# A pace and a spread: how much attention and weight work stand beside the first up projection

## The chip, the core and the metric

The kernel runs on one core of one Trainium2 chip. The metric is the device time of one execution in microseconds: the median of three runs of the kernel before is 1006.17 us (1006.15 to 1007.19). Lower is better.

## What is computed

Sliding-window attention with a linear position bias over 8 batches of 8 heads, 576 positions and head dimension 64, all float32. Its output, laid out as 4608 tokens of 512 features, is the input of a bilinear feed-forward layer.

```python
def _attn_ref(q, k, v):                      # (8, 8, 576, 64) each
    scores = scale * np.matmul(q, k.transpose(0, 1, 3, 2))
    bias = slopes[:, None, None] * (-np.abs(rel))[None, :, :]
    mask = (rel >= 0) & (rel < 128)
    scores = np.where(mask, scores + bias[None], -1e9)
    scores = scores - np.max(scores, axis=-1, keepdims=True)
    attn = np.exp(scores)
    attn = attn / (np.sum(attn, axis=-1, keepdims=True) + 1e-09)
    return np.matmul(attn, v)

def _moe_ref(x, w_a, w_b, w_out):            # (4608,512), (512,1536) twice, (1536,512)
    a = x @ w_a
    b = x @ w_b
    return a * b @ w_out
```

## The kernel before, in words

**Numbers.** TensorE multiplies float16 operands. Each float32 operand is scaled by a power of two and split into a high and a low float16 part, and a product is three matmuls (high by high, high by low, low by high). The weights arrive as 64-bit words, which the kernel first turns into float32 (`convert`, lines 126 to 136: ScalarE L130, VectorE L131 and L133, POOL L135), then squares for the norms (L141), then scales and splits (L149 and L150 for the up weights, L230 and L231 for the down weights).

**Batches.** Work is done batch by batch: the attention of a batch, four pairs of heads, then its up projection (two products per feature tile and their elementwise product), then its down projection. The attention of batch b + 1 is emitted beside the up and down projections of batch b. The attention of batch 0 runs alone at the start, beside the first steps of the weights.

**Attention as a generator.** `attention()` (line 658) goes through the pairs of batches 1 to 7. Pair i (i = 0 is the first pair of batch 1) has seven steps; after each it yields its place, i + 1/7, i + 2/7, ... i + 1. Within a pair stand: score matmuls (L374 for batch 1, L378 later) with VectorE's bias and minimum (L382) and ScalarE's exponential (L383), in four groups of 3, 2, 2 and 2 pieces; the normalization (L392, L396, ScalarE L399, VectorE L400); the DMA transpose of the probabilities on SP's queue (L405); for the pair before, the split of v (ScalarE L295, VectorE L296) and the product with v (L501), its eviction (L414) and squares (L420, L429 and POOL's addition L430); for the next pair the squares of q and k (L321), their split (L338, L339), four copies on SP's queue (L347 to L350) and the load of the pair after it (L304, L305 for batch 1; L311, L312 later). After the fourth pair of a batch its hidden state is split (L435, L436) and scaled (L515 to L522).

**Pace.** `Pace` (lines 957 to 971) runs the attention along another generator. `to(place)` steps the attention until its last yield is at or above the place; `along(main, n, place)` goes from the place where attention stands to `place` in n even parts, one at each yield of `main`:

```python
            start = max(self.at, 0)
            for k, _ in enumerate(main, 1):
                self.to(start + (place - start) * k / n)
                yield
```

**The first batch.** `first_up` (line 776) yields 48 times and once more: 12 feature tiles by two halves of the tokens by two weights, each a group of twelve matmuls (L836) into one of five PSUM banks. ScalarE copies the first product out (L783), VectorE multiplies it with the second (L785), which frees the banks; then the result is split (L829, L830, on POOL for the last six tiles). `first_down` (line 804) yields 24 times: two halves of the tokens by 12 tiles, each twelve matmuls (L812), and at the end of each half four evictions (L820, L822).

**The weights.** `up_weights` (line 165, 56 yields) and `down_weights` (line 204, 27 yields) are chained in one generator, `weights`. The first attention takes 24 of its steps. `weave` (line 949) gives a side generator `steps` steps, spread evenly over the yields a to z of the main one. The 71st step of the chain computes the scales of the down weights (L226), and each of the next twelve splits one tile of them.

**Order.** In the first batch only SP's queue keeps the order in which it is written (`manual_schedule(engines=SP)`); the other engines' instructions are put in order by the framework's scheduler, with priorities in the order of writing (a few instructions carry a higher one). From batch 1 on TensorE's order is the written one.

Of the kernel before, what the change touches and what calls it, by code (L numbers as in the profile page):

```python
# [46 lines left out]
def attention_then_bilinear_ffn(ctx: ExitStack, tc: tile.TileContext, qT, kT, vP, w_a, w_b, w_out, rel, slopes2, outT):  # L47
# [11 lines left out]
    def bank(name):  # L59

        pl = next(banks)
        return pl.tile([P, 512], F32, tag="ef" if pl is ps_ef else "ch", name=name)
# [710 lines left out]
    def new_hidden():  # L773
        return work.tile([P, 2, HT], F32, tag="rc", name="rc", bufs=3)

    def first_up(st, h):

        late = []
        hid = {}

        def keep(f, t, m, ps):
            if m == 0:
                act.copy(hid[f][:, t, :], ps[:, 0:HT])  # L783
            else:
                vec.scalar_tensor_tensor(out=hid[f][:, t, :], in0=hid[f][:, t, :], scalar=st.g, in1=ps[:, 0:HT], op0=ALU.mult, op1=ALU.mult)  # L785
                if t:
                    halve(hid.pop(f), f, h, pool if f >= NF // 2 else vec)

        for f in range(NF):
            hid[f] = new_hidden()  # L790
            for t in range(2):
                for m in range(2):
                    ps = bank("up_ps")
                    terms(ps, (f, 3 if m else 0), B12 if t else 0, True, False)
                    terms(ps, (f, 2 if m else 1), 2 if t else 1, False, True)
                    late.append((f, t, m, ps))
                    if len(late) > 2:
                        keep(*late.pop(0))
                    yield
        for x in late:  # L800
            keep(*x)
        yield

    def first_down(b, oi, h):

        started["down"] = b
        for t in range(2):
            pss = [bank("dn_ps") for _ in range(NE)]
            for f in range(NF):
                for e in range(NE):  # L810
                    for n, (wi, hi) in enumerate(((0, 0), (0, 1), (1, 0))):
                        pe.matmul(pss[e][:, 0:HT], wdn[:, f, wi, e * P:(e + 1) * P], h[:, f, t, hi, :], start=(f == 0 and n == 0), stop=(f == NF - 1 and n == 2))  # L812
                yield

            more = new_hidden()
            for e in range(NE):
                o = row() if e < 2 else more[:, e - 2, :]
                with tc.high_priority(offset=PRIO):
                    if e % 2:
                        vec.tensor_scalar(out=o, in0=pss[e][:, 0:HT], scalar1=oi, scalar2=None, op0=ALU.mult)  # L820
                    else:
                        act.activation(o, pss[e][:, 0:HT], AF.Copy, scale=oi)  # L822
                act.dma_start(outT[e * P:(e + 1) * P, b * S + t * HT:b * S + (t + 1) * HT], o)
# [4 lines left out]
    def halve(hid, f, h, eng):  # L828
        act.copy(h[:, f, :, 0, :], hid)  # L829
        eng.tensor_tensor(out=h[:, f, :, 1, :], in0=hid, in1=h[:, f, :, 0, :], op=ALU.subtract)  # L830

    def terms(ps, a, b, first, last):

        ks = [(k, wi, xi) for k in range(2) for wi, xi in ((0, 0), (0, 1), (1, 0))]
        for n, (k, wi, xi) in enumerate(ks):
            pe.matmul(ps[:, 0:HT], wup[:, a[0], a[1], wi, k, :], xs[:, b, xi, k, :], start=(first and n == 0), stop=(last and n == len(ks) - 1), skip_group_check=True)  # L836
# [104 lines left out]
    def out_scale(st):  # L941

        oi = small.tile([P, 1], F32, tag="oi", name="oi")
        vec.tensor_scalar(out=oi, in0=st.g, scalar1=smin, scalar2=so, op0=ALU.mult, op1=ALU.mult)
        vec.tensor_scalar(out=oi, in0=oi, scalar1=st.sv, scalar2=st.sv, op0=ALU.mult, op1=ALU.mult)
        vec.reciprocal(oi, oi)
        return oi

    def weave(main, *sides):

        for n, _ in enumerate(main):
            for side, a, z, steps in sides:
                if a <= n < z:
                    for _ in range((n + 1 - a) * steps // (z - a) - (n - a) * steps // (z - a)):
                        next(side, None)
# [24 lines left out]
    weights = chain(up_weights(), down_weights())  # L980
# [4 lines left out]
    h = hid.tile([P, NF, 2, 2, HT], F16, name="h")  # L985
# [8 lines left out]
    att = Pace(attention())  # L994
# [3 lines left out]

    def first_batch():
        st = states[0]  # L1000
        weave(att.along(first_up(st, h), 49, 3.2), (weights, 0, 40, 50))
        weave(att.along(first_down(0, out_scale(st), h), 24, 5.15), (weights, 0, 12, 12))
        for _ in weights:
            pass
# [9 lines left out]
    with tc.manual_schedule(engines=SP):  # L1014
        first_batch()
# [45 lines left out]
```

## Time and profile before

| | |
|---|---|
| median of three runs | 1006.17 us |
| the profiled execution's own time | 1006.95 us |
| its span | 1005.2 us |
| around the span | 1.75 us |
| first up projection (most of its matmuls) | 72.0 to 169.5 us of the span |
| first down projection | 169.5 to 215.0 us |

The span is cut into stretches, and for each the busy time of every engine is read against its length: a row of such a table gives the stretch, its length, the busy time of PE, PEld, DVE, ACT and POOL with their instructions in brackets, PEclk, the DMA share and GB/s. PE is TensorE's matmuls, PEld its weight loads, which overlap them; DVE is VectorE, ACT ScalarE, POOL GpSimd, SPq and ACTq the queues that issue transfers. PEclk is the clock granted to TensorE as a share of 2.4 GHz.

### The profile page before, as it was taken

To read this page: it belongs to the slowest core of one execution; us is meant where nothing else is said; L and a number is where in the kernel's file an instruction comes from. 1 tells how busy PE (TensorE), PEld (TensorE's weight loads), DVE (VectorE), ACT (ScalarE), POOL (GpSimd) and SP (SyncE) were. 2 spreads that over 40 slices of the span, in tenths; PEclk is the share of its full clock that TensorE was granted. 3 is DMA by queue.
4 is the path that set the end of the run, shared out by engine and by line. 5 is a ranking of instruction groups with operands and counts; after the bars stand their busy time and mean duration, and the time that the engine had idled before them with its cause. 6 is when DMAs were issued, how large, how long until landed. Compare 5 with 4: busy or idle time off the path is not lost.

```text
span 1005.2 us, 23888 instructions
## 1 busy us (share of the span) xinstructions
PE 970.8 (97%) x9339; PEld 753.6 (75%) x9339; DVE 674.8 (67%) x1833; ACT 648.9 (65%) x1715; POOL 306.1 (30%) x345
## 2 busy tenths in 40 slices
PE   8789989999999999999999999999999999999998
PEld 5557656777777777777787777777777777777776
DVE  5888999557878566785768687666677576524530
ACT  7976779657767756767767767677666766413321
POOL 3533463104565321352226112220223022211100
PEclk9889999999999999999999999999999999999999
DMA  9317733564444442462624642474425632210001
GB/s 349 120 43 269 231 114 74 120 166 80 100 90 100 137 90 43 97 172 71 121 52 105 172 90 46 93 178 103 84 57 107 163 67 43 49 37 7 2 13 36
DMA packets 148433, 102.83 MB, mean 102 GB/s; under 512 B 120032, under 2 KB 128352, under 8 KB 147296
## 3 DMA queue, kind: packets, MB, share of 16 engines
q1 hardware_dynamic: 138816, 91.77, 37.2%
q10 hardware_dynamic: 9504, 9.54, 2.9%
q8 instruction: 73, 1.20, 0.5%
q14 instruction: 40, 0.33, 0.1%
HBM read 48.33 MB, written 9.44 MB: 57 GB/s over the span
## 4 chain that ended last, share of the span: by engine, by line
PE 70%; DVE 10%; ACT 4%; DMA 2%; issue 1%; POOL 1%; SPq 0%; ACTq 0%; DVEq 0%
PE dn_ps L932 19%; PE ch L836 19%; PE p L836 14%; PE up_ps L836 10%; PE x_ps L501 4%; PE sc_ps L378 3%; DVE phl L400 2%; PE dn_ps L812 2%; DMA v<-in_vP 1%; DVE t L382 1%; DVE xs L436 1%; ACT t L383 1%; DVE wup L150 1%; ACT phl L399 1%; DVE wup L257 1%
## 5 line engine op out<-in xcount | busy, mean ns | idle before, releaser
L836 PEld LDWEIGHTS <-wup 128*128 128x128 f16 x4224 | 409.1, 98 | 120.8 <-issue 14.3
L932 PE MATMUL dn_ps<-h,wdn 128*128 128x288 f16 x2016 | 254.3, 286 | 0.0
L932 PEld LDWEIGHTS <-wdn 128*128 128x128 f16 x2016 | 193.9, 98 | 51.7
L836 PE MATMUL ch<-xs,wup 128*128 128x288 f16 x1536 | 221.5, 286 | 0.8 <-ACT rc L861 0.6
L836 PE MATMUL up_ps<-xs,wup 128*128 128x288 f16 x1536 | 197.7, 288 | 5.8 <-DVE rc L785 4.2
L836 PE MATMUL p<-xs,wup 128*128 128x288 f16 x1152 | 172.6, 286 | 0.0
L891 POOL TENSOR_TENSOR rc<-rc,row 128x288 f32<-128x288 f32 x64 | 62.3, 974 | 278.8 <-DVE row L889 262.9
L400 DVE SCALAR_TENSOR_TENSOR phl<-t,rin,phl 128x192 f16<-128x192 f32 (+2 forms) x252 | 109.5, 474 | 19.0 <-ACT phl L399 18.8
L383 ACT ACTIVATE t<-t,mn 128x192 f32<-128x192 f32 (+2 forms) x252 | 107.2, 427 | 23.3 <-DVE mn L382 23.0
L829 ACT CAST h<-rc 128x576 f16<-128x576 f32 x96 | 64.2, 669 | 68.2 <-DVE rc L896 37.6
L399 ACT ACTIVATE phl<-t,rin 128x192 f16<-128x192 f32 (+2 forms) x252 | 88.7, 425 | 23.0 <-DMA pT<-phl 10.9
L830 DVE TENSOR_TENSOR h<-rc,h 128x576 f16<-128x576 f32 x90 | 71.1, 790 | 32.7 <-ACT h L829 32.0
L382 DVE CUSTOM_DVE_ANT_0 t<-sc_ps,bias,neg 128x192 f32<-128x192 f32 (+2 forms) x216 | 73.7, 389 | 7.8 <-PE sc_ps L378 7.7
L135 POOL TENSOR_TENSOR wup<-wup,wdn 128x512 int32<-128x512 int32 x36 | 54.6, 1539 | 44.6 <-DVE wup L133 14.6
L937 ACT ACTIVATE row<-dn_ps,oi 128x288 f32<-128x288 f32 x56 | 27.6, 494 | 56.7 <-PE dn_ps L932 56.5
L873 ACT ACTIVATE row<-ch,g 128x288 f32<-128x288 f32 x64 | 31.8, 497 | 50.1 <-PE ch L836 50.1
L436 DVE TENSOR_TENSOR xs<-v,xs 128x576 f16<-128x576 f32 x52 | 48.7, 950 | 21.7 <-ACT xs L435 21.5
L360 POOL TENSOR_SCALAR bias<-rel_sb,ninv,sl_sb 128x192 f32<-128x192 f32 x24 | 21.3, 887 | 123.5 <-DVE mn L382 123.5
L868 DVE TENSOR_TENSOR rc<-p,rc 128x288 f32<-128x288 f32 x64 | 29.1, 454 | 44.4 <-PE p L836 35.0
L896 DVE SCALAR_TENSOR_TENSOR rc<-rc,g,ch 128x288 f32<-128x288 f32 x64 | 32.6, 510 | 23.8 <-PE ch L836 23.6
L383 ACT ACTIVATION_READ_ACCUMULATOR t<-t,mn 128x1 f32 x252 | 47.7, 189 | 0.0
L430 POOL TENSOR_TENSOR xq<-xq,sq 128x576 bf16<-128x576 bf16 x22 | 29.6, 1345 | 56.8 <-ACT sq L429 56.7
(151 smaller groups left out, 1315.6 us busy)
## 6 DMA issues: line engine op xcount, KB each, us to landing
v<-in_vP SPq DMA_DIRECT2D x8, 1280.0 KB, 6.5
out<-row ACTq DMA_DIRECT2D x60, 144.0 KB, 1.8
qk<-in_qT SPq DMA_DIRECT2D x28, 288.0 KB, 3.9
qk<-in_kT SPq DMA_DIRECT2D x28, 288.0 KB, 4.4
wdn<-in_w_a SPq DMA_DIRECT2D x12, 512.0 KB, 4.5
wdn<-in_w_b SPq DMA_DIRECT2D x12, 512.0 KB, 5.6
wdn<-in_w_out SPq DMA_DIRECT2D x12, 512.0 KB, 4.3
qst<-qkh SPq DMA_DIRECT2D x24, 144.0 KB, 2.7
```

Source lines behind the costliest of these rows:

```text
L135: pool.tensor_tensor(out=t[:, m, :], in0=t[:, m, :], in1=low[:, m, :], op=ALU.add)
L382: vec.tensor_tensor_reduce(out=t[:, c:c + w], in0=ps[:, c:c + w], in1=o.bias[:, WIN - w:WIN], scale=-0.125 if o.b == 1 else o.neg, scalar= ...
L383: act.activation(t[:, c:c + w], t[:, c:c + w], AF.Exp, bias=o.mn[:, n:n + 1], scale=-1.0, accum_out=o.sm[:, n:n + 1])
L399: act.activation(phl[:, 0, pc:pc + w], e, AF.Copy, scale=s)
L400: vec.scalar_tensor_tensor(out=phl[:, 1, pc:pc + w], in0=e, scalar=s, in1=phl[:, 0, pc:pc + w], op0=ALU.mult, op1=ALU.subtract)
L436: vec.tensor_tensor(out=xs[:, n, 1, :, :], in0=src, in1=xs[:, n, 0, :, :], op=ALU.subtract)
L501: pe.matmul(xp[oc // 512][64 * h:64 * h + 64, o0:o0 + w], vt[0:rows, c:c + 64], probs(pt, rows, blocks, h), start=(n == 0 and first), stop ...
L829: act.copy(h[:, f, :, 0, :], hid)
L830: eng.tensor_tensor(out=h[:, f, :, 1, :], in0=hid, in1=h[:, f, :, 0, :], op=ALU.subtract)
L836: pe.matmul(ps[:, 0:HT], wup[:, a[0], a[1], wi, k, :], xs[:, b, xi, k, :], start=(first and n == 0), stop=(last and n == len(ks) - 1), ski ...
L891: pool.tensor_tensor(out=x0, in0=x0, in1=mid, op=ALU.mult)
L932: pe.matmul(ps[:, 0:HT], wdn[:, f, wi, e * P:(e + 1) * P], h[:, f, t, hi, :], start=(m == 0 and n == 0), stop=(m == NF - 1 and n == 2))
```

## The change

One line of `first_batch` changes, in two numbers. Attention's target place beside the first up projection falls from 3.2 to 2.6 pairs; the target beside the first down projection stays at 5.15, so more of the way lies there. The fifty steps of the weights beside the first up projection are spread over its yields 0 to 44 instead of 0 to 40; the twelve beside the first down projection stay.

```diff
     def first_batch():
         st = states[0]
-        weave(att.along(first_up(st, h), 49, 3.2), (weights, 0, 40, 50))
+        weave(att.along(first_up(st, h), 49, 2.6), (weights, 0, 44, 50))
         weave(att.along(first_down(0, out_scale(st), h), 24, 5.15), (weights, 0, 12, 12))
         for _ in weights:
             pass
```

## Rows read from the trace of the kernel before

**Rows 1.** The page: busy time of each engine, share of the span, instructions.

```profile
PE 970.8 (97%) x9339; PEld 753.6 (75%) x9339; DVE 674.8 (67%) x1833; ACT 648.9 (65%) x1715; POOL 306.1 (30%) x345
```

**Rows 2.** Busy time by stretch (us; busy, then instructions), first up and first down projection.

```profile
72.00:169.50 97.50, 88.77 (x772) 65.29 (x770) 91.39 (x187) 76.01 (x168) 43.36 (x36) 0.96 0.52 168
169.50:215.00 45.50, 44.09 (x450) 33.58 (x449) 28.24 (x97) 29.19 (x89) 8.49 (x7) 1.00 0.64 135
```

**Rows 3.** The same columns, three narrower stretches of the first up projection.

```profile
95.00:104.00 9.00, 6.65 (x57) 4.73 (x57) 8.97 (x15) 6.62 (x15) 4.82 (x4) 0.94 0.86 219
125.00:134.00 9.00, 4.79 (x46) 3.23 (x45) 9.00 (x14) 6.66 (x15) 5.46 (x4) 0.98 0.35 126
134.00:142.00 8.00, 8.00 (x56) 5.49 (x54) 8.00 (x24) 8.00 (x20) 3.25 (x2) 0.81 0.34 134
```

**Rows 4.** Waits of PE, 72 to 169.5 us: total, times, longest.

```profile
PE up_ps L836 <- DVE rc L785: 4.2, 2, 2.3
```

**Rows 5.** Timeline of PE, 125 to 140 us: start, us, instruction.

```profile
129.87 1.63 PE L836 MATMUL up_ps<-xs,wup 128*128 128x288 f16 x12
133.81 3.04 PE L836 MATMUL up_ps<-xs,wup 128*128 128x288 f16 x12 [2.31 <-DVE rc L785]
```

**Rows 6.** Groups of DVE, 72 to 169.5 us: busy us, mean ns, idle before.

```profile
L400 DVE SCALAR_TENSOR_TENSOR phl<-t,rin,phl 128x192 f16<-128x192 f32 (+2 forms) x24 | 12.1, 544 | 0.0
...
L382 DVE CUSTOM_DVE_ANT_0 t<-sc_ps,bias 128x192 f32<-128x192 f32 (+2 forms) x25 | 7.3, 325 | 0.1
...
L296 DVE SCALAR_TENSOR_TENSOR vhl<-v,sv,vhl 128x640 f16<-128x640 f32 x3 | 5.7, 1922 | 1.5 <-ACT vhl L295 1.5
...
L382 DVE DVE_READ_ACCUMULATOR2_ANT mn<- 128x1 f32 x25 | 2.0, 80 | 0.0
...
L396 DVE RECIPROCAL rin<-rin 128x4 f32<-128x4 f32 (+3 forms) x5 | 0.9, 182 | 0.1
```

**Rows 7.** Groups of DVE, 169.5 to 215 us, the same columns.

```profile
L400 DVE SCALAR_TENSOR_TENSOR phl<-t,rin,phl 128x192 f16<-128x192 f32 (+2 forms) x20 | 6.9, 395 | 1.7 <-ACT phl L399 1.7
...
L296 DVE SCALAR_TENSOR_TENSOR vhl<-v,sv,vhl 128x640 f16<-128x640 f32 x1 | 0.9, 879 | 0.0
```

**Rows 8.** Timeline of all engines, 148 to 190 us.

```profile
157.51 0.29 DVE L226 TENSOR_SCALAR ratio<-sab,smin,so 128x12 f32<-128x12 f32 x1
...
159.58 1.65 PE L501 MATMUL x_ps<-pT,vhl 128*64 128x128 f16 x42
...
159.98 6.83 ACT L230 ACTIVATE wdn<-wup,ratio 128x512 f16<-128x512 f32 x11
...
164.21 0.88 PE L374 MATMUL sc_ps<-qkl,qkh 64*64 64x64 f32 x12
...
168.71 0.87 PE L374 MATMUL sc_ps<-qkl,qkh 64*64 64x192 f32 x8
...
169.54 1.75 PE L812 MATMUL dn_ps<-h,wdn 128*128 128x288 f16 x13
```

**Rows 9.** Busy time by stretch, a later one and the first down projection alone.

```profile
350.00:400.00 50.00, 49.78 (x498) 39.13 (x498) 31.37 (x87) 30.96 (x79) 10.62 (x14) 1.00 0.33 67
169.50:214.60 45.10, 43.90 (x449) 33.48 (x448) 27.84 (x96) 28.79 (x87) 8.49 (x7) 1.00 0.63 133
```

**Rows 10.** Timeline of SP's queue, 60 to 260 us.

```profile
184.00 0.65 SPq L311 DMA_DIRECT2D qk<-in_qT  x1
...
206.44 0.65 SPq L311 DMA_DIRECT2D qk<-in_qT  x1
...
208.37 5.76 SPq L405 DMA_TRANSPOSE pT<-phl  x1
214.17 0.58 SPq L268 DMA_DIRECT2D v<-in_vP  x1
```

**Rows 11.** Timeline of all engines, 216 to 240 us.

```profile
221.45 0.74 ACT L277 ACTIVATE vsq<-v 128x640 bf16<-128x640 f32 x1 [3.72 <-DMA v<-in_vP]
...
232.90 3.10 PE L836 MATMUL up_ps<-xs,wup 128*128 128x288 f16 x24 [0.41 <-ACT rc L847]
```

## The prediction

> **What bounds the kernel now.** The profile's page comes first: TensorE (PE) is busy for 97% of the span, and no other engine for more than 67% [rows 1]. So the time is TensorE's work plus the few microseconds in which it stands still, and the question is what these cost where the change is made. The table of stretches gives that: the first up projection, 72.0 to 169.5 us, holds 88.77 us of TensorE time in 97.50, so 8.7 us of idling; the first down projection behind it, 169.5 to 215.0, holds 44.09 in 45.50 [rows 2]. In the first, VectorE (DVE) is busy for 91.39 of 97.50 us, a share of 0.937; in the second it has 17 us to spare. Narrower stretches show that the two belong together: where TensorE idles most, VectorE has no gap (8.97 of 9 us, 9.00 of 9) [rows 3], and the longest total among TensorE's waits of this stage is the one for VectorE's product on line 785, which frees a PSUM bank: 4.2 us in two waits [rows 4]. After the second of these the granted clock falls to 0.81 of full speed in the stretch [rows 3], that is to the 1.2 GHz level for a part of it, and a group of twelve matmuls takes 3.04 us where the one before it took 1.63 [rows 5].
>
> **What moves.** Attention's pace yields at sevenths of a pair, and a target is met by the first yield at or above it. 3.2 is met at 3 2/7 and 2.6 at 2 5/7, so four steps change sides, 0.571 of a pair. Both versions end the first down projection at 5 2/7, so behind it nothing is moved. The four steps hold, for pair 2, the last normalization of two pieces and the DMA transpose on SP's queue; the product with v of pair 1, with its evictions, square and one POOL addition; for pair 3, five score pieces, their exponentials and one split of v; and the squares of the first pair of batch 2. All attention steps before them also slide back against the up projection, by up to 49 x 0.571 / 3.2 = 9 of its yields. SP's order is written by hand; the other four engines are ordered by the scheduler.
>
> **VectorE's relief.** Two L400 at 544 ns, five L382 at 325 and their five accumulator reads at 80, one L296 at 1922, and three short ones at 182 [rows 6]: 1.09 + 1.63 + 0.40 + 1.92 + 0.55 = 5.6 us. I take the means of the crowded stage, because with everything slid back it is average attention work that leaves its middle. The lower bound takes L400 and L296 as they run in the down projection, 395 and 879 ns [rows 7]: 0.79 + 1.63 + 0.40 + 0.88 + 0.55 = 4.2 us. If VectorE keeps its share of 0.937 the stage shortens by 5.6 / 0.937 = 6.0 us (bound: 4.5). It can't be more than the 8.7 us of idling plus the TensorE work that leaves, 3.4 us. ScalarE, at 76 us of 97.5 [rows 2], is lighter too, and its relief counts for nothing while VectorE is the tighter engine.
>
> **The clock.** If the waits of 4.2 us shrink, the slow group need not come: 3.04 - 1.63 = 1.4 us, which I take in full, since TensorE is busy for all 8.00 us of that stretch [rows 3] and so pays for it itself. Bounds: 0 and 1.4.
>
> **TensorE's own work.** The moved matmuls take 1.65 us (42 for pair 1's product), 0.88 (twelve of pair 3's scores) and 0.87 (eight more) [rows 8]: 3.4 us. They are now in the down projection, where TensorE has 1.2 us of gaps in 45.1 [rows 9], so I add 3.4 us; the 6.0 above already contain that they leave the other stage. Against this reading stands the Trainium skill, Perfetto Trace Analysis, section Identifying the Most-Contended Engine: matmul busy time overstates TensorE, and the load share of the weights (LDWEIGHTS) is the better measure. By that measure the stage has room: 33.48 of 45.10 us is 74%, against 39.13 of 50.00, 78%, later [rows 9], so 4% of 45 us, 1.8 us, would be swallowed, and the sum would be 1.8 us lower. I follow the gaps, which are counted one by one, and keep the 1.8 us as the lower end of this term.
>
> **The weights.** Fifty steps over 44 yields instead of 40. The scales of the down weights are the 47th, at yield 37.6 before and 41.4 after, of 49. Before, 11.4 yields of 1.99 us (97.5 / 49) are 22.7 us ahead of the down projection; in fact L226 ran at 157.51 and the first down matmul at 169.54 [rows 8], 12.0 us ahead, so the chain lags by 10.7. After, 7.6 yields of (97.5 - 7.4) / 49 = 1.84 us are 14.0 us, less the same lag 3.3 us. ScalarE's eleven splits take 6.83 us [rows 8], 0.62 each, and the projection uses one in twelve matmuls, so 3.3 us cover the first one and its remainder on VectorE. I cost it at nothing; if that cover goes, the down projection waits for its first weights. The loads of the weights stay ahead of the moved transpose on SP's queue (the last is the 40th step, yield 35.2 of 49), so no issue is moved past another.
>
> **The end of the down projection.** Attention now needs 5.15 - 2.714 instead of 5.15 - 3.286 of a pair in 24 yields: 0.1015 a yield, not 0.0777. The last normalization of pair 4, at 4.714, falls at yield 19.7 instead of 18.4. So 4.3 yields of (45.1 + 3.4) / 24 = 2.02 us stand behind it, 8.7 us, instead of 5.6 of 1.88, 10.5: 1.8 us later against the stage's end. Behind it, in order on SP, come the transpose, 5.76 us, and then the load of v for batch 2 [rows 10]. ScalarE's queue waits 3.72 us for that load, and TensorE 0.41 us behind ScalarE at 232.9 [rows 11]; a load that is later is paid for. I add 1.8 us (bounds: 0, if ScalarE's backlog would be there anyway, and 9.4, below).
>
> **The sum.** -6.0 - 1.4 + 3.4 + 1.8 = -2.2 us. The profiled execution took 1006.95 us, 1.75 of it around the span, and stands 0.78 above the median of the runs, 1006.17; a difference carries over, so 1004.75 for it and **1004.0 us** for the median.
>
> **The rivals.** (1) *The contention stays.* The Trainium skill, SBUF — State Buffer, section Who interferes with whom, says that a VectorE instruction with two SBUF inputs and a GpSimd instruction that reads SBUF shut each other out for a whole instruction. As a mechanism of this kernel: L400 and L296 read two SBUF operands and take 544 and 1922 ns where POOL is busy 43.36 us, and 395 and 879 where it is busy 8.49 [rows 2, 6, 7]. POOL's work on the weights doesn't move, so the lost time may stay and fall on what is left; the relief is then the lower bound, and -4.5 - 1.4 + 3.4 + 1.8 = -0.7 us gives 1005.5. (2) *The down weights come late.* A lag longer by 1.5 us than the cover gives the same 1005.5; for it, that cover is a difference of large numbers; against it, VectorE has less ahead of that chain. (3) *The change does little.* The scheduler ran eleven of twelve weight splits before the down projection began [rows 8] though nine are written beside it; if it hoists attention likewise, the time stays at 1006.2. Against it: pair 3's scores ran at 164.21 and 168.71 [rows 8], close to where they are written. (4) *Attention arrives late at batch 1, and the kernel is slower.* The loads of q and k for batch 2's pairs come 22.4 us apart, at 184.00 and 206.44 [rows 10], and each pair must pass squares, split, four copies on SP and scores before the next. At that cadence 0.571 of a pair is 12.8 us; the longer stage gives back 3.4, and 9.4 us arrive at the load of v instead of 1.8. Then -6.0 - 1.4 + 3.4 + 9.4 = +5.4 us, 1011.6. It decides from a lateness of 6.0 us on, where the sum reaches +2.0. For it: ScalarE and TensorE already wait at the end of this chain [rows 11]. Against it: TensorE paces the chain in part, which could then run closer.
>
> **How the numbers follow.** A measurement of this kernel can tell about 0.2%, 2.0 us, from no change. The forecast is the likeliest single case, 0.42: faster, though just beyond that line; its own range is 999.5 (all 8.7 us of idling gone, nothing late: -8.7 - 1.4 + 3.4 = -6.7) to 1004.1. Within 0.2%: 0.30, of which 0.12 is rival 1, 0.10 rival 2 and 0.08 rival 3. Slower: 0.28, rival 4. The range goes from 999.5 to 1010.0, which takes in a lateness of 7.8 us in rival 4 and leaves out its worst part.
>
> **What would show it.** Right: TensorE's idling in the first up projection falls from 8.7 towards 6 us, its waits for L785 shrink, no twelve matmuls take 3 us in its middle, the stage is 7 us shorter, and the down projection is some 3.4 us longer. Wrong: the up projection is as full of waits as before, the first down matmuls wait for L230 or L231, or TensorE idles between the load of v for batch 2 and some 20 us behind it.

## The result and the profile after

The changed kernel takes 1011.32 us (median of five runs, 1009.90 to 1011.78), the kernel before 1006.85 us beside it (1006.15 to 1007.19): a ratio of 1.0043, 95% interval 1.0032 to 1.0054. It is slower by 4.5 us; forecast were 1004.0 us, and the range ended at 1010.0. By its number the case that came is rival 4, whose price was 1011.6. The profiled execution has a span of 1009.4 us, 4.2 more than before. Ratios, here and below, are formed from runs made side by side and can differ by some 0.1% from the quotient of the medians.

The table of stretches of the changed kernel, first up projection, first down projection up to its last matmul, and the stretch behind it (columns as in [rows 2]):

```profile
72.00:162.50 90.50, 81.44 (x698) 61.49 (x696) 81.01 (x160) 66.84 (x144) 44.10 (x36) 0.98 0.56 175
162.50:213.90 51.40, 49.80 (x520) 36.04 (x518) 33.87 (x121) 35.39 (x103) 7.01 (x7) 1.00 0.51 112
215.00:235.00 20.00, 17.71 (x144) 13.47 (x144) 13.15 (x43) 17.15 (x51) 7.90 (x12) 0.91 0.72 194
```

Beside it two stretches of the kernel before that were not shown yet, the down projection up to its last matmul and the same 20 us behind it:

```profile
169.40:213.60 44.20, 44.00 (x451) 33.48 (x448) 26.94 (x90) 27.89 (x82) 8.49 (x7) 1.00 0.61 131
```

```profile
215.00:235.00 20.00, 19.48 (x167) 15.15 (x167) 12.27 (x42) 13.39 (x41) 9.18 (x12) 1.00 0.55 156
```

The up projection is 7.0 us shorter than in [rows 2], as forecast. Not so its idling: 90.50 - 81.44 = 9.1 us, before 8.7. It is shorter because 7.3 us of TensorE's time left it (88.77 to 81.44), and the down projection took that over, 44.2 to 51.4 us long. Its last matmul starts at 213.5 us; before, at 213.2. So up to here the change is worth nothing, and most of the 4.2 us arise behind. The waits of PE in the changed up projection (total, times, longest):

```profile
PE up_ps L836 <- DVE wup L133: 3.0, 1, 3.0
PE wn_ps L156 <- ACT wdn L141: 2.7, 2, 2.3
PE up_ps L836 <- DVE rc L785: 1.9, 1, 1.9
PE up_ps L836 <- ACT rc L783: 1.4, 1, 1.4
```

The wait for L785 did shrink, from 4.2 [rows 4] to 1.9. In its place TensorE waits for the conversion of the weights. L141 squares a set of up weights whose norms (L156) are next. The L133 is another matter, as its timeline and TensorE's show:

```profile
140.24 2.18 DVE L133 SCALAR_TENSOR_TENSOR wup<-wdn,wup 128x1024 int32<-128x1024 int32 x1
```

```profile
142.48 11.16 PE L836 MATMUL up_ps<-xs,wup 128*128 128x288 f16 x79 [2.98 <-DVE wup L133]
```

This is the seventeenth L133 of eighteen, and the sets from the thirteenth on are down weights. Their float32 form is kept in parts 4 and 5 of the tile `wup` until it is split (line 87), while L836 reads parts 0 to 3. So TensorE stands for 3.0 us before the 38th of its 48 groups for values that it doesn't read. That L133 writes parts of feature tiles 8 and 9 at once, and the parts of tile 9 that the group reads lie between the two; it is likely that the framework takes that for an overlap, but no run tests it. VectorE's groups of that stretch (busy, mean ns) show that it has shed more than the forecast's 5.6 us, 91.39 to 81.01, and that this was not what TensorE waited for:

```profile
L133 DVE SCALAR_TENSOR_TENSOR wup<-wdn,wup 128x1024 int32<-128x1024 int32 x10 | 15.3, 1526 | 0.1
L150 DVE SCALAR_TENSOR_TENSOR wup<-wup,sup 128x512 f16<-128x512 f32 x13 | 13.6, 1057 | 0.5 <-ACT wup L149 0.5
...
L400 DVE SCALAR_TENSOR_TENSOR phl<-t,rin,phl 128x192 f16<-128x192 f32 (+2 forms) x17 | 7.7, 502 | 0.6 <-ACT phl L399 0.6
```

What left the up projection on TensorE is seen in PE's groups of the first up projection, before and then after:

```profile
L836 PE MATMUL up_ps<-xs,wup 128*128 128x288 f16 x557 | 74.1, 292 | 4.7 <-DVE rc L785 4.2 <-ACT rc L783 0.5
L374 PE MATMUL sc_ps<-qkl,qkh 64*64 64x192 f32 (+2 forms) x108 | 11.2, 332 | 0.7 <-DVE mn L382 0.7
L501 PE MATMUL x_ps<-pT,vhl 128*64 128x128 f16 (+3 forms) x84 | 3.5, 230 | 0.0
```

```profile
L836 PE MATMUL up_ps<-xs,wup 128*128 128x288 f16 x553 | 71.8, 289 | 6.3 <-DVE wup L133 3.0 <-DVE rc L785 1.9 <-ACT rc L783 1.4
L374 PE MATMUL sc_ps<-qkl,qkh 64*64 64x192 f32 (+2 forms) x80 | 7.8, 318 | 0.0
...
L501 PE MATMUL x_ps<-pT,vhl 128*64 128x128 f16 (+3 forms) x42 | 1.7, 229 | 0.0
```

28 score matmuls (3.4 us) and 42 products with v (1.8 us) are 5.2 us of attention; some 2.3 us are L836, with four records fewer in the stretch and fewer of its matmuls at the 1.2 GHz level (0.98 of the clock granted, 0.96 before). The end of the down projection, in PE's timeline, before and after:

```profile
214.63 0.19 PE L515 MATMUL n_ps<-xq,ones 128*128 128x64 bf16 x1 [1.14 <-ACT row L822]
215.10 1.63 PE L836 MATMUL up_ps<-xs,wup 128*128 128x288 f16 x12 [0.28 <-DVE row L820]
```

```profile
217.29 0.21 PE L515 MATMUL n_ps<-xq,ones 128*128 128x64 bf16 x1 [3.50 <-ACT row L822]
217.32 3.06 PE L836 MATMUL up_ps<-xs,wup 128*128 128x288 f16 x12
```

TensorE stands still for 3.5 us instead of 1.1, waiting for the eviction on line 822, and the first twelve matmuls of batch 1 then take 3.06 us instead of 1.63: the granted clock of the stretch is 0.91, so part of it at the 1.2 GHz level. Those two, 2.4 and 1.4 us, and the 0.3 from before, less the wait of 0.28 us for L820 that is gone, leave TensorE 3.6 us behind at its next matmul (L332 at 220.18, before at 216.57). After that the distance lies between 2.6 and 4.3 us, and it is 4.2 at the end. What L822 stands behind is told by the chain of waits of the changed kernel (start, us, piece):

```profile
188.68 9.88 DMA pT<-phl
...
198.65 0.36 ACT phl L399
...
201.49 1.26 ACT qkh L338
...
204.84 0.72 DVE xs L436
205.56 3.52 DMA qst<-qkl
...
210.31 4.46 DMA qk<-in_kT
...
214.88 1.26 ACT qkl L321 x2
...
216.86 0.39 ACT row L822
217.25 0.04 issue
217.29 0.21 PE n_ps L515
```

It is attention, without a gap, from the transpose of pair 3 on: the transpose frees the buffer that the next normalization writes; behind that come the split, the copies on SP, the load of k and its squares, and ScalarE takes the eviction only after these. Before, other work stands in the same place: the squares (L321) ahead of the eviction wait for TensorE's own scores, after the change for the load of k.

```profile
211.62 1.16 ACT L321 ACTIVATE qkl<-qk 128x1152 bf16<-128x1152 f32 x1 [3.74 <-PE sc_ps L378]
```

```profile
214.88 1.16 ACT L321 ACTIVATE qkl<-qk 128x1152 bf16<-128x1152 f32 x1 [4.19 <-DMA qk<-in_kT]
```

So, as the traces have it, the 1.1 us before are what follows the last scores in TensorE's own order, and the 3.5 us are attention's lateness.

### The profile page after: what moved, and what is told of

Same layout as the page of the kernel before. It is cut to its first block, busy times and chain, and to the rows that moved or that the text cites. A ratio compares the mean times of both kernels' runs of the same rounds, so it can differ in the third digit from the quotient of the medians.

```text
span 1009.4 us, 23896 instructions
## 1 busy us (share of the span) xinstructions
PE 972.0 (96%) x9339; PEld 754.3 (75%) x9339; DVE 671.6 (67%) x1833; ACT 649.1 (64%) x1715; POOL 304.9 (30%) x345
## 4 chain that ended last, share of the span: by engine, by line
PE 71%; DVE 11%; DMA 8%; ACT 7%; issue 2%; SPq 0%; POOL 0%; ACTq 0%; DVEq 0%; POOLq 0%
PE ch L836 18%; PE dn_ps L932 16%; PE p L836 13%; PE up_ps L836 12%; PE x_ps L501 5%; PE sc_ps L378 3%; DMA pT<-phl 3%; DVE phl L400 2%; PE dn_ps L812 2%; DMA wdn<-in_w_b 2%; DVE wup L150 1%; DMA qk<-in_kT 1%; DMA v<-in_vP 1%; ACT phl L399 1%; DVE xs L436 1%
## 5 line engine op out<-in xcount | busy, mean ns | idle before, releaser
L836 PEld LDWEIGHTS <-wup 128*128 128x128 f16 x4224 | 409.5, 98 | 123.6 <-issue 13.3
L836 PE MATMUL ch<-xs,wup 128*128 128x288 f16 x1536 | 221.6, 286 | 1.3 <-ACT rc L861 0.7
L836 PE MATMUL up_ps<-xs,wup 128*128 128x288 f16 x1536 | 196.9, 288 | 6.8 <-DVE wup L133 3.0
L836 PE MATMUL p<-xs,wup 128*128 128x288 f16 x1152 | 172.7, 286 | 0.0
L400 DVE SCALAR_TENSOR_TENSOR phl<-t,rin,phl 128x192 f16<-128x192 f32 (+2 forms) x252 | 108.9, 473 | 16.2 <-ACT phl L399 16.0
L399 ACT ACTIVATE phl<-t,rin 128x192 f16<-128x192 f32 (+2 forms) x252 | 88.7, 425 | 26.3 <-DMA pT<-phl 12.6
L501 PE MATMUL x_ps<-pT,vhl 128*64 128x128 f16 (+3 forms) x1176 | 46.8, 229 | 1.3 <-DVE cl L107 0.8
```

What stands on the lines that cost most here:

```text
L399: act.activation(phl[:, 0, pc:pc + w], e, AF.Copy, scale=s)
L400: vec.scalar_tensor_tensor(out=phl[:, 1, pc:pc + w], in0=e, scalar=s, in1=phl[:, 0, pc:pc + w], op0=ALU.mult, op1=ALU.subtract)
L501: pe.matmul(xp[oc // 512][64 * h:64 * h + 64, o0:o0 + w], vt[0:rows, c:c + 64], probs(pt, rows, blocks, h), start=(n == 0 and first), stop ...
```

## The experiments

The expectations name theories by letters. On the up projection: V, the forecast's, has VectorE's load from attention set its idling; P has POOL's additions on line 135 do it. On the late end of the down projection: S blames the weights' spread, W a single queue in front of the eviction, C the stores that collide with the transpose, and L the chain of attention, which has a length of its own and now starts too late.

**The two numbers apart.** On one chip, with the two runs that follow these; the kernel before took 1008.38 us there.

```diff
-        weave(att.along(first_up(st, h), 49, 2.6), (weights, 0, 44, 50))
+        weave(att.along(first_up(st, h), 49, 2.6), (weights, 0, 40, 50))
```

> Pace target 2.6 alone, the weights again over 40 yields. Theory W (the wait): most of the loss of the changed kernel is one TensorE wait of 3.5 us at the end of the first down projection, for an eviction that stands on ScalarE behind squares that wait for the load of q and k, and the 1.4 us of slow clock behind it. Theory O (overfull): the down projection beside which attention was put is full, so each moved piece of work costs its length, and no single wait matters. Theory S (spread): the later weights do it. W and O: 1009 to 1012 us, as the changed kernel. S: within 2 us of the kernel before, 1006.9.

1018.2 us, ratio 1.0104 (1.0090 to 1.0118). Its up projection and its waits there and in the down projection:

```profile
72.00:167.50 95.50, 84.87 (x728) 63.37 (x724) 87.47 (x172) 70.83 (x154) 41.41 (x35) 0.98 0.54 169
```

```profile
PE up_ps L836 <- DVE wup L133: 4.6, 1, 4.6
PE dn_ps L812 <- DVE row L820: 3.4, 1, 3.4
PE wn_ps L156 <- ACT wdn L141: 2.6, 2, 1.9
```

That is more than any of the three theories had. With the pace alone TensorE idles 10.6 us in the up projection: relieved of attention, it only comes sooner to the weights' conversions, the seventeenth L133 above all.

```diff
-        weave(att.along(first_up(st, h), 49, 2.6), (weights, 0, 44, 50))
+        weave(att.along(first_up(st, h), 49, 3.2), (weights, 0, 44, 50))
```

> Weights over 44 yields alone, pace target 3.2 as before. W and O: within 2 us of the kernel before, 1005 to 1009 us, since the attention stands where it stood. S: 1010 to 1012 us, as the changed kernel, with waits of the first down matmuls for the splits of the down weights.

1009.33 us, ratio 1.0009 (1.0000 to 1.0018), and the wait at the end is 1.1 us as before, though TensorE idles 11.6 us in the up projection, 3.1 of it for the seventeenth L133. The spread by itself costs next to nothing, and beside the slower pace it gives back 0.6%. The harm is the pace's.

**Another engine for the eviction.**

```diff
-                    if e % 2:
+                    if e % 2 or t:
```

> The changed kernel, with all four evictions of the second half of the first down projection on VectorE (L820); TensorE's order is that of the changed kernel. W: the wait of 3.5 us falls under 1 us and the slow group of matmuls behind it runs at full clock, so 3 to 5 us less than the changed kernel, 1006.5 to 1008.5. O: the same time as the changed kernel, 1010 to 1012. S: the same as O.

1010.33 us, ratio 1.0025 (1.0012 to 1.0037). The wait fell only from 3.5 to 2.9 us and was then for VectorE's eviction (L820); the twelve matmuls behind it took 1.63 us. So W was right about the slow group and not about the wait: ScalarE's queue by itself is not the cause.

**Less attention before the end.**

```diff
-        weave(att.along(first_down(0, out_scale(st), h), 24, 5.15), (weights, 0, 12, 12))
+        weave(att.along(first_down(0, out_scale(st), h), 24, 5.0), (weights, 0, 12, 12))
```

> The changed kernel, with the target beside the first down projection at 5.0 instead of 5.15, so that the last two attention steps (five or four score pieces and the squares that wait for the load) move to the up projection of batch 1. W: the squares no longer stand before the eviction, the wait of 3.5 us goes, 1006 to 1009 us. O: the stage gets about 1 us shorter by the TensorE work that leaves, and the next one longer by as much: 1010 to 1012 us.

1016.37 us, ratio 1.0082 (1.0067 to 1.0097). The wait for the eviction is gone, and the time is above what any theory had; PE's longest waits between 200 and 235 us are now those of scores in and behind the end of the projection:

```profile
PE sc_ps L378 <- DMA qkh<-qkh: 3.4, 1, 3.4
PE sc_ps L378 <- DVE mn L382: 2.2, 1, 2.2
```

Moved past the end, the late work is waited for one step on: what is late is the chain and not one instruction in it.

**The change again, and two links put elsewhere**, on another chip (before: 1008.3 us).

> The changed kernel unaltered, as the measure for the runs beside it on one chip: 0.3 to 0.6% above the kernel before; TensorE's wait for an eviction at the end of the first down projection 3 to 4 us, the DMA transpose of pair 3 (the one that starts near 189 us) 9 to 11 us to landing.

The change, unaltered: 1012.45 us, ratio 1.0039 (1.0027 to 1.0051), wait 3.5 us. In this execution the up projection is 92.2 us long with 84.48 of TensorE, so 7.7 us of idling: over two executions it is 7.7 and 9.1, against 8.7 before.

```diff
-                act.dma_start(outT[e * P:(e + 1) * P, b * S + t * HT:b * S + (t + 1) * HT], o)
+                (act.dma_start if t else lambda *x: held.append(x))(outT[e * P:(e + 1) * P, b * S + t * HT:b * S + (t + 1) * HT], o)
...
-                yield
+                yield [act.dma_start(*x) for x in held if f == 4]
```

> The changed kernel with the four output stores of the first half of the first down projection (0.59 MB) issued four yields into the second half; the orders of TensorE and SP are those of the changed kernel. Theory C (collision): at 2.6 the transpose at place 4.0 falls together with these stores, so it takes 9.9 us to land instead of 7.6, and ScalarE's queue is held 2.9 us by issuing them; normalization, product with v, copies and the next load are all that much later, and the wait of 3.5 us at the end is this lateness. C: the transpose lands in 6.5 to 8 us, the wait at the end is under 1.5 us, no slow group behind it, and the time is 2.5 to 5 us below the changed kernel. Theory L (chain too long anyway): the chain of 22 us per pair doesn't fit into the shortened way with or without these stores; the wait at the end stays at 2.5 us or more and the time within 1 us of the changed kernel.

1012.61 us, ratio 1.0035 (1.0023 to 1.0047). A miss: the scheduler issued the stores where they had been, at 191.5 to 194.8 us, and the run tells nothing of C.

```diff
-            lay_out(nxt)
-            load(i + 2)
+            load(i + 2) if i == 4 else lay_out(nxt)
+            lay_out(nxt) if i == 4 else load(i + 2)
```

> The changed kernel with the load of q and k for pair 6 issued on SP ahead of the four copies of pair 5, not behind them; TensorE's order is that of the changed kernel. It can start when the split has read the tile, some 3 us earlier. If the last wait is ScalarE standing before the evictions on squares that wait for this load, the load lands 2 to 4 us earlier, the wait of 3.5 us shrinks to 0 to 1.5, the slow group behind it goes, and the time falls by 2 to 4 us, unless the copies, now 1.3 us later, make the scores of pair 5 wait. If something else holds the evictions, the wait stays.

1013.18 us, ratio 1.0057 (1.0040 to 1.0075). The load went 4 to 5 us earlier and the wait of 3.5 us vanished; in its place the scores waited 1.5 us for the copies, the last twelve down matmuls behind them took 2.98 us, and 16 us into batch 1 TensorE waited another 1.5 us for ScalarE (L847). The lateness moved again.

**POOL's additions.** The kernel before, with the lowest bits left out of the weights from the seventh converted set on:

```diff
-        for m in range(2):
+        for m in range(2 if n < 6 else 0):
             pool.tensor_tensor(out=t[:, m, :], in0=t[:, m, :], in1=low[:, m, :], op=ALU.add)
```

> The kernel before, without POOL's addition of the low words (L135) from the seventh weight tile on, which leaves the lowest bits of those weights out. It asks what the 8.7 us of TensorE idling in the first up projection are. Theory P (the chain of the weights through POOL, and POOL's contention with VectorE): TensorE idles under 5 us in this stage, L150 takes 0.75 us instead of a mean of 1.2, and the time falls by 3 to 7 us. Theory V (VectorE's load as such, which attention adds to): idling of 7 us or more stays.

994.31 us, ratio 0.9864 (0.9849 to 0.9878). The up projection ends at 154.4 us and idles 1.7; its stretch and three of VectorE's groups:

```profile
72.00:154.40 82.40, 80.73 (x733) 61.51 (x731) 69.67 (x175) 71.31 (x162) 13.82 (x13) 1.00 0.61 199
```

```profile
L150 DVE SCALAR_TENSOR_TENSOR wup<-wup,sup 128x512 f16<-128x512 f32 x11 | 8.0, 751 | 0.9 <-ACT wup L149 0.9
L400 DVE SCALAR_TENSOR_TENSOR phl<-t,rin,phl 128x192 f16<-128x192 f32 (+2 forms) x20 | 7.6, 425 | 0.4 <-ACT phl L399 0.4
...
L296 DVE SCALAR_TENSOR_TENSOR vhl<-v,sv,vhl 128x640 f16<-128x640 f32 x4 | 3.5, 883 | 0.9 <-ACT vhl L295 0.9
```

At the pace of before (84 score matmuls fall into the stretch, where 108 did) the idling is nearly gone: P, though the gain of 14 us is twice what P had. L400 and L296 stand at 425 and 883 ns, against 544 and 1922 [rows 6], near the 395 and 879 of the down projection [rows 7]. The Trainium skill, SBUF — State Buffer, section Who interferes with whom, says that a VectorE instruction with two SBUF inputs and a GpSimd instruction that reads SBUF exclude each other; the trace agrees, in that both lines, which read two SBUF tiles, shorten by these amounts when half of POOL's additions go.

**The same edit on the changed kernel, the additions moved, the stores left out, a target between**, on one chip (before: 1007.94 us).

> The changed kernel with the addition of the weights' lowest bits on POOL left out from the seventh converted set on (as in the run that did it to the kernel before: those weights lack their lowest bits). Theory P (the up projection idles on POOL's additions and on what they take from VectorE; how much attention stands in it makes no difference to the idling): idle time in the up projection 1 to 3 us, as there; what is left of the change is the work moved and the lateness behind it, so this is 2 to 6 us slower than the kernel before with the same edit (994.3). Theory V (the forecast's: VectorE's load from attention makes the idling, and its relief pays once the rest is out of the way): 2 to 5 us faster than that one.

1005.61 us, ratio 0.9973 (0.9960 to 0.9985), so the change now costs 11 us. Its up projection idles 6.0 us, 5.3 of them in one wait for L133 where the run above had no wait over 1.0; the down projection is 52 us long (45 there), and the wait at its end 3.2 us (1.5 there). V falls: with the other limit taken away, less attention beside the up projection helps nothing. P's numbers are missed too, idling of 1 to 3 us and a cost of 2 to 6, by that one wait and by the down projection.

The kernel before with the additions on VectorE:

```diff
-            pool.tensor_tensor(out=t[:, m, :], in0=t[:, m, :], in1=low[:, m, :], op=ALU.add)
+            (pool if n < 6 else vec).tensor_tensor(out=t[:, m, :], in0=t[:, m, :], in1=low[:, m, :], op=ALU.add)
```

> The kernel before with those same additions on VectorE instead of POOL (24 additions of 128x512, nothing left out). An addition on VectorE should take some 0.65 us, half of what the 128x1024 combination takes there with little beside it (1.22 us), so 20 of them put some 13 us on VectorE in the up projection. Theory P: what POOL's additions took from VectorE (21.7 us less busy without them) is more than that, the idle time falls from 8.7 to 2 to 6 us, and the ratio is 0.988 to 0.996. Theory V: VectorE's load sets the idling, it is over its share already (0.937), and 13 us more on it make the stage longer: ratio over 1.003.

1005.64 us, ratio 0.9976 (0.9963 to 0.9988). Two of VectorE's groups and the stretches of up and down projection:

```profile
L135 DVE CUSTOM_DVE_ANT_0 wup<-wdn,wup 128x1024 uint16<-128x1024 uint16 x20 | 13.5, 711 | 0.1
L133 DVE SCALAR_TENSOR_TENSOR wup<-wdn,wup 128x1024 int32<-128x1024 int32 x10 | 12.1, 1210 | 0.0
```

```profile
72.00:162.30 90.30, 84.07 (x744) 62.54 (x743) 81.16 (x201) 73.03 (x164) 14.36 (x14) 0.96 0.57 181
162.30:213.60 51.30, 46.97 (x457) 35.31 (x456) 29.13 (x94) 29.90 (x87) 7.40 (x7) 0.97 0.54 113
```

VectorE does 13.5 us more and is still 10.2 us less busy than in [rows 2], and the stage is 7.1 us shorter. No wait for VectorE is left in it: the 6.2 us of idling, just over P's 2 to 6, are one wait of a product with v for ScalarE's split of v (L295). Whether the idling of before went with VectorE's longer instructions or with the longer way of each set through POOL (1579 ns an addition for 711) these two runs don't separate. But the down projection is as much longer, 4.3 us of it idle, and ends where it ended: TensorE waits for two transposes. The gain is smaller than P had it, since it assumed that a shorter up projection is kept.

The changed kernel without the first half's stores:

```diff
-                act.dma_start(outT[e * P:(e + 1) * P, b * S + t * HT:b * S + (t + 1) * HT], o)
+                (act.dma_start if t else lambda *x: 0)(outT[e * P:(e + 1) * P, b * S + t * HT:b * S + (t + 1) * HT], o)
```

> The changed kernel without the four output stores of the first half of the first down projection (they are left out, so the first half of batch 0 is missing from the output); the order of work on TensorE and on the sync engine's queue is that of the changed kernel. Theory C (the transpose of pair 3 collides with these stores: it lands in 9.9 us, 7.6 before, and ScalarE's queue is held by their issue): the transpose lands in 6.5 to 8 us, the wait of n_ps for ScalarE's row at the end of the first down projection falls from 3.5 to under 1.5 us, its twelve slow matmuls of 3.06 us go, and the kernel is 2.5 to 5 us shorter than the changed one (some 1.5 of it may come from the transfers left out themselves): ratio to the kernel before 0.999 to 1.002. Theory L (the chain of attention in the first down projection is late because 44 columns' work starts from further behind; stores have no part in it): the transpose may land sooner, but the wait stays at 2.5 us or more, and the ratio at 1.003 or more.

1011.55 us, ratio 1.0024 (1.0013 to 1.0036), between what C and L gave, and not clear of the changed kernel's 1.0032 to 1.0054; the wait is still 3.5 us, but the twelve matmuls behind it take 1.63 us. The transpose lands in 8.3 us, 1.6 less than beside the stores, and from the first down matmul (164.5) to batch 1 it takes 53.0 us instead of 54.7 (54.4 in the repeat). So in this execution the collision costs some 1.5 us of the projection's length; its end moves with the transpose, so the wait stays.

A target between, as a difference from the kernel before:

```diff
-        weave(att.along(first_up(st, h), 49, 3.2), (weights, 0, 40, 50))
+        weave(att.along(first_up(st, h), 49, 2.9), (weights, 0, 42, 50))
```

> A target between: 2.9 instead of 2.6 (before 3.2), the weights' steps over 0 to 42. The place of the transpose then lies before the end of the first half of the down projection, clear of its stores, and about half of the attention is moved. Theory C: the wait at the end of the down projection is under 2 us as before, and the ratio is 0.997 to 1.002. Theory L: the lateness is half as large, the wait is 2 to 3 us, and the ratio 1.001 to 1.004. Both: the idle time of TensorE in the up projection stays at 8 to 10 us.

1013.31 us, ratio 1.0044 (1.0031 to 1.0058). Half the step costs as much as the whole: the wait is 3.7 us, and TensorE idles 10.7 us in the up projection. The stores, issued from 192.9 to 194.8 us, still meet the transpose (188.6 to 197.3), which lands in 8.7 us, so the run wasn't the clean test of C that it was meant to be; but with a shorter collision the wait is no shorter. L had it smaller too.

**A link left out, and the mirror of the change**, on one chip (before: 1007.8 us).

```diff
-        sp.dma_start(o.qs[0:64, :, :], hi[0:64, :, :])
-        sp.dma_start(o.qs[64:128, :, :], lo[0:64, :, :])
...
+        copy = sp.dma_start if (b, p) != (2, 1) else lambda *x: 0
+        copy(o.qs[0:64, :, :], hi[0:64, :, :]), copy(o.qs[64:128, :, :], lo[0:64, :, :])
...
```

> The changed kernel without the four copies on the sync engine's queue that lay out one pair (the second of batch 2, issued at 204.96 to 209.1 us there); its scores are computed from the pair before, so that part of the attention of batch 2 is wrong, and nothing else is taken away. Theory L (the chain behind the transpose of pair 3 holds batch 1 back): the load of k behind the copies is issued some 3.7 us earlier, the squares on ScalarE with it, the wait of 3.5 us of n_ps for ScalarE's row falls under 1 us, the slow group of 3.06 us behind it goes to 1.6, and the kernel is 3 to 4.5 us shorter than the changed one: ratio to the kernel before 0.999 to 1.002. Rival (what holds ScalarE is something else that ends at the same time, as its exponentials or the product on VectorE): the wait stays over 2.5 us and the ratio over 1.003.

1012.24 us, ratio 1.0048 (1.0033 to 1.0063), wait 3.0 us: L's number is missed. ScalarE's timeline shows why the run doesn't settle it:

```profile
210.88 1.16 ACT L321 ACTIVATE qkl<-qk 128x1152 bf16<-128x1152 f32 x1 [3.84 <-DMA qk<-in_kT]
...
213.50 1.49 ACT L399 ACTIVATE phl<-t,rin 128x192 f16<-128x192 f32 x4 [0.25 <-DVE rin L396]
216.28 0.35 ACT L383 ACTIVATE t<-t,mn 128x64 f32<-128x64 f32 x1 [1.29 <-DVE mn L382]
...
217.01 0.48 ACT L822 ACTIVATE row<-dn_ps,oi 128x288 f32<-128x288 f32 x1
```

The squares (L321) came 4 us earlier, as L said, but the scheduler now put them ahead of the normalization on ScalarE's queue, which then waited 3.84 us for the load. The work between is the same and so is its end.

The mirror, as a difference from the kernel before:

```diff
-        weave(att.along(first_up(st, h), 49, 3.2), (weights, 0, 40, 50))
+        weave(att.along(first_up(st, h), 49, 3.7), (weights, 0, 40, 50))
```

> The kernel before with the target of 3.2 raised to 3.7 instead of lowered, the weights as before: the mirror of the change. Theory L: the transposes stand earlier against the end of the down projection, batch 1 starts 27 to 30 us behind that of pair 3 or, if TensorE is then the later of the two, right behind the last down matmul; the wait for ScalarE's row is under 1.2 us; TensorE has 3 to 6 us more work in the up projection and as much less in the down projection, so the ratio is 0.997 to 1.003. Theory V (VectorE's load in the up projection sets its idling): idle time there rises from 8.7 to 11 us or more, and the ratio is 1.002 to 1.006.

1010.27 us, ratio 1.0023 (1.0014 to 1.0032): inside L's bounds and inside V's, with 12.6 us of idling in the up projection. But 3.3 of these are a wait for a transpose, 3.0 are for the seventeenth L133, and only 3.0 are for L785.

> The same with the 24 additions on VectorE instead of POOL, where the up projection was 7 us shorter and the down projection gave all 7 back, 4.3 us of it as idle time of TensorE behind two transposes. Theory L: with more attention beside the up projection the transposes come earlier, that idle time falls under 2 us, and the ratio is 0.992 to 0.997. Rival (the down projection is 51 us long there for another reason): idle time there stays at 3 us or more, and the ratio is at 0.998 or above.

1006.61 us, ratio 0.9989 (0.9980 to 0.9997): neither in full. The idling left the down projection (0.1 us) and turned up ahead of it, in the up projection's waits:

```profile
PE x_ps L501 <- DMA pT<-phl: 5.5, 1, 5.5
PE up_ps L836 <- DVE wup L133: 3.5, 1, 3.5
```

**All runs together.** Us of the profiled span; the transpose is the one of pair 3, batch 1 the first matmul behind the down projection that isn't one of its own, the last column the time from the transpose to it.

| run | first down matmul | transpose | last down matmul | batch 1 | from the transpose |
|---|---|---|---|---|---|
| before | 169.5 | 185.6 | 213.2 | 214.6 | 29.0 |
| after | 162.6 | 188.7 | 213.5 | 217.3 | 28.6 |
| pace only | 167.5 | 198.0 | 222.1 | 225.9 | 27.9 |
| spread only | 170.5 | 188.7 | 215.6 | 217.0 | 28.3 |
| evictions on VectorE | 165.5 | 191.6 | 216.3 | 219.4 | 27.8 |
| change again | 164.2 | 190.3 | 214.9 | 218.6 | 28.3 |
| stores later (no effect) | 164.2 | 190.2 | 215.3 | 218.9 | 28.7 |
| load before copies | 163.9 | 189.9 | 218.2 | 218.4 | 28.5 |
| half the additions | 154.4 | 172.3 | 199.2 | 201.0 | 28.7 |
| the same, changed | 156.3 | 183.8 | 208.1 | 211.6 | 27.8 |
| additions on VectorE | 162.4 | 185.9 | 213.2 | 214.5 | 28.6 |
| no first stores | 164.5 | 190.6 | 213.6 | 217.5 | 26.8 |
| target 2.9 | 169.0 | 188.6 | 214.1 | 218.0 | 29.5 |
| no copies | 163.8 | 189.8 | 214.3 | 217.5 | 27.7 |
| down target 5.0 | 164.0 | 192.2 | 216.3 | 216.4 | 24.2 |
| mirror, 3.7 | 178.0 | 186.3 | 217.8 | 218.9 | 32.6 |
| mirror, VectorE | 174.8 | 182.2 | 214.6 | 215.7 | 33.5 |

Where the target is at most 3.2 in the up projection and 5.15 in the down projection, batch 1 starts 26.8 to 29.5 us behind that transpose, wherever the down projection began (154 to 171 us) and the transpose stood (172 to 198). With less attention before the end it is 24.2, and the wait follows later; with the mirror more TensorE work lies behind the transpose than that, and the wait at the end is 0.8 us. This is a regularity over the first fourteen rows, and no more: that the chain behind the transpose makes it is what the chain of waits of the changed kernel says and three edits agree with (load before copies, target 5.0, no copies: each moved the lateness and none took it away). In three of the rows it is something else: before, half the additions and additions on VectorE have the last squares wait for TensorE's scores, so their 28.6 to 29.0 us aren't made by attention's chain alone. No run shortened that chain in one place with the order on ScalarE unchanged, so it isn't shown by itself.

The wait for L133 has a plainer rule. In these three runs it is absent; in all others TensorE waits 2.3 to 5.3 us, and the wait ends 0.05 to 0.07 us behind the seventeenth L133 (with half the additions and the change the eighteenth; there the scheduler has put that set last, hence the 5.3). The group that waits is the 38th where the spread ends at yield 44 and the 37th where it ends at 40 or 42.

## Why the prediction was wrong

**VectorE's relief (-6.0): the number met, the reason wrong.** "If VectorE keeps its share of 0.937 the stage shortens by 6.0" is the step that failed. The share fell to 81.01 / 90.50 = 0.895 and the idling stayed. The row that was read rightly, VectorE without a gap where TensorE waits [rows 3], doesn't tell what fills it: 21.7 us of its 91.4 went when POOL's additions did, most of it the same instructions running shorter, and TensorE's idling fell from 8.7 to 1.7. Attention beside them was only what the waits happened to end on. Of the 9.1 us after the change 3.0 are the wait for the seventeenth L133, which no term of the prediction has. Rival 1 named the mechanism and still charged the relief at its lower bound of 4.2 / 0.937; as far as idling goes it was 0.

**The clock (-1.4): not kept.** In the first execution more of the up projection's TensorE time ran at the upper level (2.3 us less for L836), but slow matmuls came in its middle all the same, behind the wait for L133 (0.68 granted from 140 to 145 us). In the repeat even that gain is gone: 0.96 granted and 292 ns for L836, as before. At the end of the down projection a group at the lower level came on top, +1.4.

**TensorE's work (+3.4): mis-sized, 7.2.** 70 matmuls changed sides, for which I had 62. By groups they are 5.2 us in the up projection, where some stood at the lower level (eight scores took 1.54 us at 103.2 us, with 0.78 granted from 100 to 105, and not 0.87). The down projection grew by 7.2: 5.8 us of TensorE (49.80 against 44.00) and 1.4 more idling. The Trainium skill, Perfetto Trace Analysis, section Identifying the Most-Contended Engine, calls matmul busy time no good measure of how close TensorE is to its roofline and judges its room by the load share of the weights. The trace doesn't show such room here: with a load share of 74% [rows 9] the stage grew by all that was moved into it and more.

**The end (+1.8): mis-sized, and taken at the wrong link.** It came to 2.4 us of wait and 1.4 of clock. The step took the lateness of the last normalization, at place 4.71. The chain that sets the end begins at place 4.0, with the transpose of pair 3. By the step's own method this lies at yield 9.2 before and 12.7 after; behind it are 14.8 yields of 1.83 us (44.0 / 24), 27 us, and after 11.3 of 2.13 (51.2 / 24), 24 us. Against a chain of some 28 us that is 4 us too little after the change, near the wait of 3.5. This is reckoned afterwards, with the chain's length taken from the table, and it explains the changed kernel alone: before, the wait of 1.1 us hangs on TensorE's scores and not on this chain.

**Rival 4** had the side and the time (1011.6 for 1011.3) with chance 0.28. That the time fits so well is luck: its 9.4 us of lateness came to 3.8, and its sum has 3.4 us for the down projection's growth of 7.2. Its place was another, too: the last transpose beside the up projection is 9.7 us late (155.90 for 146.23), about the 9.4 it reckoned; 6.4 of these are made up by the next one, and the last 3 never, since both kernels take some 15 and then some 22.5 us between the transposes that follow. TensorE stops at the eviction and not behind the load of v. **The weights** held as far as the forecast went: no down matmul waits for L230 or L231. The step that no issue is moved past another did not: two loads of weights now go ahead of a transpose (97.76 and 98.63 us) that stood before them (96.71 and 103.43). What a conversion did hold up was the up projection, which the forecast left out of account. **Rivals 2 and 3** didn't occur.

## What to carry to other kernels

Before work is shifted between two stages by a pace, find the longest dependent chain in the receiving stage, take the place where it starts, and set the time left behind that place against its length; the last step of the chain told too little here. An engine without gaps is not yet the bound: ask what its instructions would take without their neighbour (here 425 for 544 ns, 883 for 1922), and remove the neighbour before the load. A wait for an instruction is not yet a need for its result: look up which set it was and whether the waiting work reads it. And a stage that gets shorter is worth something only if the next stage isn't tied to a chain that starts earlier: with the additions on VectorE the up projection gained 7.1 us, and 2.3 us (1007.94 - 1005.64) reached the end.

## What the runs showed of the hardware

- An addition that POOL does in 1579 ns for 128x512 (twenty of them 31.1 us) takes VectorE 711 ns for the same piece, and moving it there lowered VectorE's own busy time by 10.2 us in the stage: L150 went from 1205 to 742 ns and the one-input L131 from 938 to 684.
- A DMA transpose that lands in 7.6 us with no store beside it (kernel before) took 9.9 beside four output stores of 144 KB, and 8.3 with these left out. The stores slowed too, from medians of 1.9 and 3.2 us to landing to 6.3 and 6.1, and two store issues held ScalarE's queue for 2.74 us where they had taken 0.91:

```profile
191.87 2.74 ACTq L823 DMA_DIRECT2D out<-rc  x2
194.66 0.35 ACT L383 ACTIVATE t<-t,mn 128x64 f32<-128x64 f32 x1 [2.87 <-issue]
```
